# Local-score normalisation and expert-score scaling on VectorE instead of GpSimd

## The chip, the cores and the metric

The kernel runs on one core of one Trainium2 chip. The metric is device time in microseconds (us) of one execution; the median of three runs stands for a kernel.

## The reference

Three layers run one after the other on a batch of 4 sequences of 768 tokens. The first is a local attention with 8 heads of 64: each chunk of 32 queries sees 8 memory keys, 16 keys to the left, its own 32 and 8 to the right. The second is a mixture of four causal attention experts over the 512 outputs of the first; each token keeps its two best experts by a gate. The third is a low-rank mix over the sequence followed by a feed-forward block of 2048.

```
scores = scale * np.matmul(q_c, k_full.transpose(0, 1, 3, 2))
scores = scores - np.max(scores, axis=-1, keepdims=True)
a = np.exp(scores)
a = a / (np.sum(a, axis=-1, keepdims=True) + 1e-09)      # local attention
...
a = np.exp(scores)                                       # expert e, causal, 768 x 768
a /= a.sum(-1, keepdims=True) + 1e-09
ye = a @ v @ wo[e]
...
out += mask[..., None] * w[:, :, kk:kk + 1] * ye         # the token's two gates
...
u = x + h.transpose(0, 2, 1)                             # h = low-rank mix
ch = np.maximum(u @ w_ch1, 0.0) @ w_ch2
```

## The kernel before

**Stages.** From the start to about 450 us of the profiled span the core runs both attentions, interleaved; behind that come the feed-forward products. The change touches the first stage alone.

**Rounds.** `rnd` writes one round of the attention. It takes up to three pieces of work: the scores of one expert block (`scores`: batch `b`, pair of experts `pr`, block `i` of 128 queries against `(i+1)*128` keys), the values of the block of the round before (`turn_scores`, `values`), the scores of one local unit (`local_load`, `local_scores`: a pair of heads and half a sequence, in two groups `qd` of three windows) and the turning and values of the local unit of the round before (`local_turn`, `local_values`). There are 12 rounds for each of the 4 batches, and 6 rounds ahead of them with local units alone. Projections (`qk_proj`, `v_proj`) fill the rounds. In the last batch the first steps of the feed-forward block (`fuse_w1`, `load_w2`, `early`) fill them too.

**Chain of one local group.** TensorE writes three score tiles of 128x96 (line 417). VectorE adds the band and takes the minimum (line 421), ScalarE takes the exponential with its sum `ss` (line 424), VectorE makes `rs = 1/(ss + 1e-9)` (lines 427 and 428), GpSimd multiplies the 128x288 tile `a` by `rs` (line 429). One round later TensorE transposes `a` (line 437), VectorE or ScalarE copies it out of PSUM (line 439) and TensorE multiplies by the values (line 665). There are 64 such groups.

**Chain of one expert block.** TensorE writes the scores of two experts (lines 548, 549, 551). VectorE takes the maximum (lines 566 or 575), ScalarE the exponential with its sum `su` (line 560), VectorE makes `1/(su + 1e-9)` (lines 579, 580), GpSimd multiplies each of the two tiles `ac` (128 by 128 to 768) by it and by the token's gate (line 582). One round later TensorE transposes it (line 600), the copies `ath` out of PSUM (line 603) alternate between ScalarE and VectorE, and TensorE multiplies by the values (line 665). There are 48 blocks, so 96 scalings. The gate `g` (lines 519 to 535) is made on VectorE, eight times.

**What else GpSimd and VectorE do there.** GpSimd also copies the halves `kd`, `kl` of the expert keys to the other partitions (line 496, 64 times). VectorE also makes the low parts `xl` of the local outputs (line 456), on which the projections wait, `qs` and `kl` (lines 488, 494), and the output of the mix, `z` (line 657).

**What sets the order.** The program text is written round by round; the framework's scheduler then gives each engine one queue in a fixed order, by priority and a model of durations, and the engines meet through semaphores. An instruction that waits holds all that is behind it on its engine. Only the runs of narrow matmuls (`part`, line 665) are kept together by explicit dependencies. PSUM is short: `s` and `tp` share two buffers, `sc`, `tpc`, `pyt`, `pz` share another two.

Of the kernel before, what the change touches and what calls it, by code (L numbers as in the profile page):

```python
# [22 lines left out]
GK = NMEM + LEFT + GQ + RIGHT  # L23
# [69 lines left out]
def tile_chunk_attention__moe_attention__mixer(  # L93
# [19 lines left out]
    nc = tc.nc  # L113
# [217 lines left out]
    with ExitStack() as p1:  # L331
# [77 lines left out]
        def local_scores(u, qd):  # L409
            b, hp, hf = u  # L410
            w = half[u]
            s = ps.tile([128, 3, GK], F32, name="s", **TL)
            a = lwk.tile([128, 3, GK], F32, name="a")
            nm = sm.tile([128, 3], F32, name="nm")
            ss = sm.tile([128, 3], F32, name="ss")
            for j in range(3):
                nc.tensor.matmul(s[:, j, :], w["q"][:, qd * 3 + j], w["k"][:, qd * 3 + j], start=True, stop=True)  # L417
            for j in range(3):
                g = hf * NG // 2 + qd * 3 + j
                bd = band_s[:, 0 if g == 0 else 2 if g == NG - 1 else 1]  # L420
                nc.vector.tensor_tensor_reduce(a[:, j, :], s[:, j, :], bd, op0=ALU.add, op1=ALU.min,  # L421
                                               scale=-scale, scalar=-NEG_LOCAL, accum_out=nm[:, j:j + 1])
            for j in range(3):
                nc.scalar.activation(a[:, j, :], a[:, j, :], AF.Exp, bias=nm[:, j:j + 1], scale=-1.0,  # L424
                                     accum_out=ss[:, j:j + 1])
            rs = sm.tile([128, 3], F32, name="rs")
            nc.vector.tensor_scalar(rs, ss, 1e-9, None, op0=ALU.add)
            nc.vector.reciprocal(rs, rs)  # L428
            nc.gpsimd.tensor_mul(a, a, rs[:, :, None].to_broadcast([128, 3, GK]))  # L429
            w["a"][qd] = a  # L430

        def local_turn(u, qd):
# [108 lines left out]
        def score_mm(s, off, b, e, i, base):  # L541

            q = qs[b, e, i // 3][:, i % 3 * 128:(i % 3 + 1) * 128]
            for hf in range(i // 3 + 1):
                w = HALF if hf < i // 3 else (i % 3 + 1) * 128
                o = off if hf == 0 else base
                last = hf == i // 3
                nc.tensor.matmul(s[:, o:o + w], q, kl[b, e, hf][:, :w], start=True, stop=False)  # L548
                nc.tensor.matmul(s[:, o:o + w], q, kd[b, e, hf][:, :w], start=False, stop=not last)  # L549
                if last:  # L550
                    nc.tensor.matmul(s[:, o + w - 128:o + w], identb_s, tri_s, start=False, stop=True)

        def scores(b, pr, i, between=None):
            n = (i + 1) * 128
            nm = sm.tile([128, 2], F32, name="nmc")
            su = sm.tile([128, 2], F32, name="su")
            aa = [cw.tile([128, S], F32, name="ac", bufs=NAC) for _ in range(2)]

            def expo(h, src):
                nc.scalar.activation(aa[h][:, :n], src, AF.Exp, bias=nm[:, h:h + 1], scale=1.0, accum_out=su[:, h:h + 1])  # L560

            if i < 3:
                s = ps.tile([128, 2, 512], F32, name="sc", **TC)
                for h in range(2):
                    score_mm(s[:, h], 0, b, 2 * pr + h, i, 0)
                nc.vector.tensor_reduce(nm, s[:, :, :n], axis=AX.X, op=ALU.max, negate=True)
                for h in range(2):
                    expo(h, s[:, h, :n])
                if between:
                    between()  # L570
            else:
                for h in range(2):
                    s = ps.tile([128, 1024], F32, name="sc", **TC)
                    score_mm(s, 128, b, 2 * pr + h, i, 512)
                    nc.vector.tensor_reduce(nm[:, h:h + 1], s[:, 128:128 + n], axis=AX.X, op=ALU.max, negate=True)  # L575
                    expo(h, s[:, 128:128 + n])
                    if h == 0 and between:
                        between()
            nc.vector.tensor_scalar(su, su, 1e-9, None, op0=ALU.add)
            nc.vector.reciprocal(su, su)  # L580
            for h in range(2):
                nc.gpsimd.tensor_scalar(aa[h][:, :n], aa[h][:, :n], su[:, h:h + 1],  # L582
                                        gates[b, i // 3][:, i % 3, 2 * pr + h:2 * pr + h + 1], op0=ALU.mult, op1=ALU.mult)
            a_ts[b, pr, i] = aa

# [83 lines left out]
        def rnd(new=None, old=None, s_unit=None, o_unit=None, fill1=(), fill2=(), down=None):  # L669
            if s_unit:  # L670
                local_load(s_unit)
                local_scores(s_unit, 0)
# [6 lines left out]
            if new:  # L679
                scores(*new, between)  # L680
            if not turned:
                between()
            if s_unit:
                local_scores(s_unit, 1)
# [96 lines left out]
        for b in range(B):  # L781
# [7 lines left out]
            for r, (pr, i) in enumerate(ROUNDS):  # L789
                n = (FILL0 if b == 0 else FILL)[r] if work else 0  # L790
# [263 lines left out]
```

## Time and profile before

| | us |
|---|---|
| median of 3 runs | 863.04 (862.87 to 864.9) |
| the profiled execution | 859.0 |
| its span, first to last instruction | 857.2 |
| TensorE busy with matmuls | 811.0 (95%) |
| VectorE busy | 630.5 (74%) |
| ScalarE busy | 494.8 (58%) |
| GpSimd busy | 168.0 (20%) |

The mean granted TensorE clock is 0.984 of full speed. Busy time is the share of the span in which an engine executes. A share of the whole span mixes stages; the section of rows gives the engines by stage. GpSimd's 168.0 us lie almost wholly in the first 450 us.

### The profile page before, as it was taken

To read this page: it belongs to the slowest core of one execution; us is meant where nothing else is said; L and a number is where in the kernel's file an instruction comes from. 1 tells how busy PE (TensorE), PEld (TensorE's weight loads), DVE (VectorE), ACT (ScalarE), POOL (GpSimd) and SP (SyncE) were. 2 spreads that over 40 slices of the span, in tenths; PEclk is the share of its full clock that TensorE was granted. 3 is DMA by queue.
4 is the path that set the end of the run, shared out by engine and by line. 5 is a ranking of instruction groups with operands and counts; after the bars stand their busy time and mean duration, and the time that the engine had idled before them with its cause. 6 is when DMAs were issued, how large, how long until landed. Compare 5 with 4: busy or idle time off the path is not lost.

```text
span 857.2 us, 18057 instructions
## 1 busy us (share of the span) xinstructions
PE 811.0 (95%) x6404; PEld 727.1 (85%) x6404; DVE 630.5 (74%) x1997; ACT 494.8 (58%) x1464; POOL 168.0 (20%) x254
## 2 busy tenths in 40 slices
PE   7889999999999998889979999999999999999995
PEld 5778999889987897768767878999989989899995
DVE  5687766577767766899536899989578495775947
ACT  3587766577656755656434566656464454645533
POOL 5334343344433424222110000000000000000002
PEclk8799999999999999999999999999999999999999
DMA  9644422133222201253206744301203012030101
GB/s 246 181 122 112 111 76 75 57 98 107 50 68 76 85 1 45 86 182 108 74 19 200 226 159 148 99 25 50 75 1 123 1 50 75 1 124 1 62 38 50
DMA packets 59627, 74.74 MB, mean 87 GB/s; under 512 B 29456, under 2 KB 34064, under 8 KB 58768
## 3 DMA queue, kind: packets, MB, share of 16 engines
q1 hardware_dynamic: 59536, 73.57, 27.9%
q8 instruction: 51, 0.84, 0.4%
q14 instruction: 40, 0.33, 0.1%
HBM read 57.83 MB, written 15.73 MB: 86 GB/s over the span
## 4 chain that ended last, share of the span: by engine, by line
PE 72%; DVE 9%; DMA 8%; ACT 6%; issue 3%; SPq 1%; POOL 1%; DVEq 0%; ACTq 0%; POOLq 0%
PE acc L934 23%; PE ph L285 14%; PE t L665 7%; PE pqk L468 5%; DMA raw<-in_w 4%; PE pv L508 3%; PE s L417 3%; PE tpc L600 3%; PE po L301 3%; PE sc L548 3%; PE sc L549 2%; PE tp L437 2%; DMA part<-o 2%; ACT a L424 1%; ACT ac L560 1%
## 5 line engine op out<-in xcount | busy, mean ns | idle before, releaser
L934 PE MATMUL acc<-xhi,sw 128*128 128x256 f32 x1008 | 191.6, 283 | 0.9 <-ACT xhi L876 0.9
L934 PEld LDWEIGHTS acc<-xhi,sw 128*128 128x128 f32 x1008 | 160.6, 189 | 8.1 <-ACT xhi L876 2.2
L934 PE MATMUL acc<-xlo,sw 128*128 128x256 f32 x504 | 139.2, 283 | 0.0
L873 DVE TENSOR_TENSOR sx<-t 128x256 f32<-128x256 f32 x180 | 67.8, 420 | 72.0 <-ACT t L866 72.0
L866 ACT ACTIVATE t<-ph 128x512 f32<-128x512 f32 x72 | 43.0, 597 | 121.2 <-PE ph L285 121.2
L582 POOL TENSOR_SCALAR ac<-ac,su,g 128x128 f32<-128x128 f32 (+5 forms) x96 | 70.0, 738 | 157.7 <-DVE su L580 102.7
L934 PEld LDWEIGHTS acc<-xlo,sw 128*128 128x128 f32 x504 | 95.4, 189 | 2.6
L925 POOL TENSOR_TENSOR pt<-pt,cp 128x512 f32<-128x512 f32 x3 | 6.4, 2155 | 408.6 <-DVE xlo L877 408.6
L876 ACT CAST xhi<-sx 128x256 fp32r<-128x256 f32 x210 | 76.0, 407 | 13.8 <-PE acc L934 6.2
L424 ACT ACTIVATE a<-a,nm 128x96 f32<-128x96 f32 x192 | 69.9, 367 | 22.9 <-DVE nm L421 22.2
L877 DVE TENSOR_TENSOR xlo<-sx,xhi 128x256 fp32r<-128x256 f32 x210 | 80.1, 421 | 3.8 <-ACT xhi L876 3.3
L560 ACT ACTIVATE ac<-sc,nmc 128x128 f32<-128x128 f32 (+5 forms) x96 | 60.4, 632 | 35.3 <-DVE nmc L575 20.3
L285 PE MATMUL ph<-zh,wp_l 128*128 128x512 f32 x192 | 61.0, 398 | 1.0 <-ACT zh L273 1.0
L417 PE MATMUL s<-k_t,qbd 128*128 128x96 f32 x384 | 56.3, 284 | 5.3 <-DMA k_t<-in_kw 4.0
L600 PE MATMUL tpc<-ident_s,ac 128*128 128x128 f32 x336 | 54.0, 279 | 7.0 <-ACT ath L603 2.9
L285 PE MATMUL ph<-zh,wp_h 128*128 128x512 f32 x192 | 60.3, 394 | 0.0
L429 POOL TENSOR_TENSOR a<-a,rs 128x288 f32<-128x288 f32 x64 | 42.6, 668 | 82.1 <-DVE rs L428 23.2
L417 PEld LDWEIGHTS s<-k_t,qbd 128*128 128x128 f32 x384 | 51.2, 200 | 8.1 <-issue 4.0
L285 PE MATMUL ph<-zl,wp_h 128*128 128x512 f32 x176 | 56.6, 393 | 0.0
L548 PE MATMUL sc<-kl,qs 128*128 128x384 f32 (+2 forms) x144 | 51.3, 357 | 2.6 <-DVE z L657 1.4
L421 DVE CUSTOM_DVE_ANT_0 a<-s,band_s 128x96 f32<-128x96 f32 x192 | 40.2, 252 | 16.6 <-PE s L417 13.9
L600 PEld LDWEIGHTS tpc<-ident_s,ac 128*128 128x128 f32 x336 | 39.5, 143 | 13.0 <-issue 6.2
(174 smaller groups left out, 2038.7 us busy)
## 6 DMA issues: line engine op xcount, KB each, us to landing
raw<-in_w SPq DMA_DIRECT2D x64, 256.0 KB, 3.5
k_t<-in_kw SPq DMA_DIRECT2D x32, 288.0 KB, 3.4
v_t<-in_vw SPq DMA_DIRECT2D x32, 288.0 KB, 3.2
qbd<-in_qT SPq DMA_DIRECT2D x64, 96.0 KB, 2.8
part<-o SPq DMA_DIRECT2D x24, 256.0 KB, 2.5
pt<-part SPq DMA_DIRECT2D x6, 1024.0 KB, 4.9
out<-pt SPq DMA_DIRECT2D x24, 256.0 KB, 2.5
zf<-zs SPq DMA_DIRECT2D x8, 512.0 KB, 4.7
```

What stands on the lines that cost most here:

```text
L285: nc.tensor.matmul(p, w[f // 4][:, pr, fs], z[:, pr], start=(n == 0), stop=(n == 5))
L417: nc.tensor.matmul(s[:, j, :], w["q"][:, qd * 3 + j], w["k"][:, qd * 3 + j], start=True, stop=True)
L424: nc.scalar.activation(a[:, j, :], a[:, j, :], AF.Exp, bias=nm[:, j:j + 1], scale=-1.0, accum_out=ss[:, j:j + 1])
L548: nc.tensor.matmul(s[:, o:o + w], q, kl[b, e, hf][:, :w], start=True, stop=False)
L560: nc.scalar.activation(aa[h][:, :n], src, AF.Exp, bias=nm[:, h:h + 1], scale=1.0, accum_out=su[:, h:h + 1])
L582: nc.gpsimd.tensor_scalar(aa[h][:, :n], aa[h][:, :n], su[:, h:h + 1], gates[b, i // 3][:, i % 3, 2 * pr + h:2 * pr + h + 1], op0=ALU.mult, ...
L600: nc.tensor.transpose(tp[h][:, j * 128:(j + 1) * 128], aa[h][:, j * 128:(j + 1) * 128], ident_s)
L665: session.append(nc.tensor.matmul(*a, **kw).ins)
L873: nc.vector.tensor_tensor(x, t[:, p[0], p[1]], t[:, q[0], q[1]], op=op)
L876: nc.scalar.copy(hi, x)
L877: nc.vector.tensor_sub(lo, x, f32(hi))
L934: nc.tensor.matmul(acc[n][:, m], w[:, ms], x, start=(f == FA and u == 0 and m == 0), stop=(f == NF - 2 and u == 2 and m == 1))
```

## The change

Two instructions change engine. The multiplication of the local scores by the reciprocal of their sum, and the scaling of the expert scores by reciprocal and gate, are issued on VectorE with the same operands.

```
@@ -426,7 +426,7 @@
             rs = sm.tile([128, 3], F32, name="rs")
             nc.vector.tensor_scalar(rs, ss, 1e-9, None, op0=ALU.add)
             nc.vector.reciprocal(rs, rs)
-            nc.gpsimd.tensor_mul(a, a, rs[:, :, None].to_broadcast([128, 3, GK]))
+            nc.vector.tensor_mul(a, a, rs[:, :, None].to_broadcast([128, 3, GK]))
             w["a"][qd] = a
@@ -579,7 +579,7 @@
             nc.vector.tensor_scalar(su, su, 1e-9, None, op0=ALU.add)
             nc.vector.reciprocal(su, su)
             for h in range(2):
-                nc.gpsimd.tensor_scalar(aa[h][:, :n], aa[h][:, :n], su[:, h:h + 1],
+                nc.vector.tensor_scalar(aa[h][:, :n], aa[h][:, :n], su[:, h:h + 1],
                                         gates[b, i // 3][:, i % 3, 2 * pr + h:2 * pr + h + 1], op0=ALU.mult, op1=ALU.mult)
             a_ts[b, pr, i] = aa
```

Since the scheduler orders the queues anew, other instructions shift too. GpSimd's queue keeps its other work in the order it had. Two places on VectorE's queue show what happens. The first is the end of the sixth gate, at 266 to 269 us of the trace of before (`g_4116`, `den_4128` are the gate; `a_4213`, `rs_4225`, `rs_4307` belong to local groups, `su_4065` and `ac_` to an expert block; + is after, - is before):

```order
 L579 TENSOR_SCALAR su_4065<-su_4065 128x2
 L530 SCALAR_TENSOR_TENSOR g_4116<-cnt_4125,g_4116 128x12
+L429 TENSOR_TENSOR a_4213<-a_4213,rs_4225 128x288
 L580 RECIPROCAL su_4065<-su_4065 128x2
+L532 TENSOR_REDUCE den_4128<-g_4116 128x3
 L427 TENSOR_SCALAR rs_4307<-ss_4297 128x3
-L532 TENSOR_REDUCE den_4128<-g_4116 128x3
+L582 TENSOR_SCALAR ac_4066<-ac_4066,su_4065,g_3524 128x128
+L582 TENSOR_SCALAR ac_4067<-ac_4067,su_4065,g_3524 128x128
+L533 TENSOR_SCALAR den_4128<-den_4128 128x3
 L428 RECIPROCAL rs_4307<-rs_4307 128x3
```

The multiplications stand between the small steps of the gate, and the copy `at_4233` (line 439), which stood ahead of `rs_4225` before, stands behind `rs_4307` now.

The second is a little ahead of it, in the queue in front of `xl_3945`, a low part on which a projection waits:

```order
+L579 TENSOR_SCALAR su_3949<-su_3949 128x2
+L580 RECIPROCAL su_3949<-su_3949 128x2
+L582 TENSOR_SCALAR ac_3950<-ac_3950,su_3949,g_3524 128x384
+L582 TENSOR_SCALAR ac_3951<-ac_3951,su_3949,g_3524 128x384
 L456 TENSOR_TENSOR xl_3945<-t_3927,xh_3944 128x384
-L566 TENSOR_REDUCE nmc_3948<-sc_3952 128x2
 L421 ISA a_4213,nm_4214<-s_4212,band_s_106 128x96
```

The reciprocal of this block and both its scalings were moved ahead of `xl_3945` and of the local minimum of `s_4212`.

## Rows read from the trace of the kernel before

**Rows 1.** Busy us, share and instructions of each engine, from the page.

```profile
PE 811.0 (95%) x6404; PEld 727.1 (85%) x6404; DVE 630.5 (74%) x1997; ACT 494.8 (58%) x1464; POOL 168.0 (20%) x254
```

**Rows 2.** Busy time by stage: from:to, length, engines, granted clock, DMA share, GB/s.

```profile
core 0: us, PE busy (x) PEld busy (x) DVE busy (x) ACT busy (x) POOL busy (x), PEclk, DMA share, GB/s
43.00:364.00 321.00, 304.39 (x3083) 277.50 (x3082) 231.61 (x926) 214.60 (x750) 124.83 (x200) 1.00 0.27 78
364.00:450.00 86.00, 77.52 (x502) 62.08 (x500) 60.68 (x140) 44.01 (x107) 16.28 (x18) 0.96 0.29 95
450.00:857.00 407.00, 394.16 (x2608) 359.66 (x2606) 312.45 (x815) 215.88 (x526) 6.39 (x3) 1.00 0.23 79
```

**Rows 3.** The chain that ended last, shares of the span, from the page.

```profile
PE 72%; DVE 9%; DMA 8%; ACT 6%; issue 3%; SPq 1%; POOL 1%; DVEq 0%; ACTq 0%; POOLq 0%
```

**Rows 4.** The chain, 43 to 364 us: start, us, what (DVE's ends, POOL's pieces).

```profile
43.94 0.26 DVE a L421
...
100.53 0.67 POOL a L429
...
102.56 1.53 POOL ac L582 x2
...
360.48 0.34 DVE d_t L129
```

**Rows 5.** Lines 429, 582: min/median/max ns; who waited for them; page group (idle before last).

```profile
L429 POOL TENSOR_TENSOR a<-a,rs x64: 664/666/700, 12.6 to 302.3; 128x288 f32<-128x288 f32 x64
...
  PEld tp L437: 0.5, 1
```

```profile
L582 POOL TENSOR_SCALAR ac<-ac,su,g x96: 442/764/1576, 64.2 to 434.2; 128x128 f32<-128x128 f32 x16, 128x256 f32<-128x256 f32 x16, 128x384 f32<-128x384 f32 x16, 128x512 f32<-128x512 f32 x16
...
  DVE a L421: 1.0, 1
  PEld tpc L600: 0.5, 2
```

```profile
L582 POOL TENSOR_SCALAR ac<-ac,su,g 128x128 f32<-128x128 f32 (+5 forms) x96 | 70.0, 738 | 157.7 <-DVE su L580 102.7
```

**Rows 6.** VectorE instructions of like shape: count, busy us, mean ns, idle before.

```profile
L877 DVE TENSOR_TENSOR xlo<-sx,xhi 128x256 fp32r<-128x256 f32 x210 | 80.1, 421 | 3.8 <-ACT xhi L876 3.3
L970 DVE TENSOR_TENSOR pt<-pt,acc 128x512 f32<-128x512 f32 x22 | 14.5, 681 | 0.0
L603 DVE COPY ath<-tpc 128x768 f32<-128x768 f32 x8 | 7.6, 954 | 6.0 <-PE tpc L600 6.0
L603 DVE COPY ath<-tpc 128x128 f32<-128x128 f32 x8 | 2.3, 284 | 3.9 <-PE tpc L600 3.9
```

**Rows 7.** Casts on VectorE from one SBUF tile, line 366: min/median/max ns.

```profile
L366 DVE CAST wqk_h<-raw x4: 426/508/1118, 4.3 to 10.2; 128x512 fp32r<-128x512 f32 x4
L366 DVE CAST wvg_h<-raw x4: 297/298/694, 14.0 to 18.5; 128x260 fp32r<-128x260 f32 x4
```

**Rows 8.** Multiplications and scalings by stage: POOL's busy us (instructions), lines 429, 582.

```profile
43.00:364.00 321.00, 35.94 (x54) 1.00 0.27 78
```

```profile
43.00:364.00 321.00, 56.15 (x82) 1.00 0.27 78
```

**Rows 9.** Line 427 on VectorE: its group with the mean; its min/median/max.

```profile
L427 DVE TENSOR_SCALAR rs<-ss 128x3 f32<-128x3 f32 x64 | 16.0, 250 | 14.9 <-ACT a L424 14.7
```

```profile
L427 DVE TENSOR_SCALAR rs<-ss x64: 140/170/1192, 11.2 to 301.8; 128x3 f32<-128x3 f32 x64
```

**Rows 10.** The timeline at 267 us: start, us, engine, line (POOL, then DVE).

```profile
267.22 0.67 POOL L429 TENSOR_TENSOR a<-a,rs 128x288 f32<-128x288 f32 x1 [1.51 <-DVE g L530]
```

```profile
267.31 0.60 DVE L427 TENSOR_SCALAR rs<-ss 128x3 f32<-128x3 f32 x1
```

**Rows 11.** A wait of the whole span: us in total, times, longest.

```profile
PEld t L665 <- DVE ath L603: 8.2, 11, 1.9
```

**Rows 12.** Busy time from 364 to 407 us, columns as in group 2.

```profile
364.00:407.00 43.00, 40.40 (x226) 32.22 (x225) 39.91 (x99) 26.62 (x67) 11.06 (x12) 0.96 0.44 144
```

More of the change, by code (lines that the diff above doesn't have):

```diff
@@ L428, in local_scores @@
             nc.vector.reciprocal(rs, rs)
-            nc.gpsimd.tensor_mul(a, a, rs[:, :, None].to_broadcast([128, 3, GK]))
+            nc.vector.tensor_mul(a, a, rs[:, :, None].to_broadcast([128, 3, GK]))
             w["a"][qd] = a
@@ L581, in scores @@
             for h in range(2):
-                nc.gpsimd.tensor_scalar(aa[h][:, :n], aa[h][:, :n], su[:, h:h + 1],
+                nc.vector.tensor_scalar(aa[h][:, :n], aa[h][:, :n], su[:, h:h + 1],
                                         gates[b, i // 3][:, i % 3, 2 * pr + h:2 * pr + h + 1], op0=ALU.mult, op1=ALU.mult)
```

## The prediction

> **What bounds the kernel now.** I read the busy times first, then the same by stage, then the chain of work that ended last, then the two lines that change. TensorE is busy 95% of the span [rows 1]. By stage it is 304.4 of 321 us from 43 to 364, 77.5 of 86 us from there to 450, and 394.2 of 407 us behind [rows 2]. So TensorE is the bound, and all that the attention could give back between 43 and 450 us is its idle time, 16.6 + 8.5 = 25.1 us. GpSimd is busy 124.8 of the 321 us and VectorE 231.6, or 72% [rows 2]. Of the chain, 72% of the span is on TensorE, 9% on VectorE and 1% on GpSimd [rows 3]. Between 43 and 364 us I added up its pieces: 141 on VectorE, from the one at 43.94 to the one at 360.48, are 40.8 us, 12.7% of the stretch; the multiplications on GpSimd are two pieces, 0.67 and 1.53 us [rows 4]. VectorE is thus the second engine of the path and GpSimd hardly on it. That shows from the other side too: TensorE's weight loads waited for line 429 once, 0.5 us, and for line 582 twice, 0.5 us, and VectorE waited for line 582 once, 1.0 us [rows 5]. GpSimd itself mostly waits: it was idle 157.7 us ahead of line 582, 102.7 of it until a reciprocal of line 580 [rows 5]. One round lies between these products and the transposes that read them, and this round covers GpSimd's slowness.
>
> **What goes from GpSimd.** The 64 multiplications have a median of 666 ns, the 96 scalings one of 764 ns [rows 5]. Nearly all of it was cover. What can be given back on the path is the two pieces, 2.2 us, since VectorE's own time for them is counted below.
>
> **What comes to VectorE.** The trace has no such instruction on VectorE, so I bound it by its likes. A multiplication has two inputs in SBUF: 256 columns take 421 ns and 512 columns, one input from PSUM, 681 ns [rows 6], or 1.016 ns for each column more, so 288 columns make 421 + 32 x 1.016 = 453 ns; 64 of them are 29.0 us. A scaling reads one SBUF tile. The casts from one SBUF tile take 298 ns for 260 columns and 426 ns at best for 512 [rows 7], 0.51 ns a column; from 128 to 768 columns this is 230, 296, 361, 426, 491 and 557 ns, 2,361 ns in sum, and 16 of each are 37.8 us. The upper end is a copy that reads PSUM, 284 ns for 128 columns and 954 for 768 [rows 6]; on a straight line between them the six sizes make 3,714 ns, and 16 of each 59.4 us. I take 37.8, since casts share source and destination with the scalings, and keep 59.4 for the range. Together VectorE gets 66.8 us. Between 43 and 364 us there are 54 of the 64 and 82 of the 96 [rows 8], 24.5 us and, by GpSimd's time for them, 37.8 x 56.15 / 70.0 = 30.3 us (70.0 us in all, [rows 5]): 54.8 us.
>
> **What VectorE gets back.** Line 427, the addition on 128x3, has a median of 170 ns but a mean of 250 and a worst case of 1192 [rows 9]. The timeline shows why: at 267.31 it takes 0.60 us, beginning just behind a GpSimd multiplication of 0.67 us and ending with it [rows 10]. A small VectorE instruction on SBUF tiles stands still while GpSimd works. The excess is 64 x 80 ns = 5.1 us for this line. Other lines on SBUF tiles show the same now and then, and the copies of line 496 stay on GpSimd and go on doing it, so I take 5 to 10 us in all, 8 for the sum. Page SBUF — State Buffer, section Who interferes with whom, of the Trainium skill says that the two engines share a port pair, which a VectorE instruction with two SBUF inputs or in a two-port mode and a GpSimd instruction hold in turn, each for its whole length. By that rule, the trace agrees where small instructions meet GpSimd, and both kinds of new instruction would be among those that can be held up by the copies of line 496; I have no row for that, and leave it to the upper end.
>
> **What of it lies on the path.** From 43 to 364 us VectorE goes from 231.6 to 231.6 + 54.8 - 8 = 278 us, 87% of the stretch; its idle time halves, from 89 to 43 us. A piece laid on VectorE at random hits a stretch where the path is on VectorE 12.7% of the time as things are; with half the idle time left to absorb it, I let the rate double to 25% by the last piece and take the mean, 19%: 54.8 x 0.19 = +10.4 us. If the rate stayed it would be +7.0. The hits are of a kind that exists already: the copies `ath` make TensorE's weight loads wait 8.2 us in 11 places now [rows 11], and the two scalings in front of `xl` hold up 2 x 0.36 us what a projection waits for. No new wait for another engine comes with the change: each product needs only the reciprocal ahead of it on its own queue, and `a` and `ac`, whose sums VectorE had waited for already. What queues behind it is the next minimum, maximum, copy or low part, and TensorE behind that. Off go the 2.2 us of GpSimd on the path, and of the 8 us given back the part that lay on it: six pieces of line 427 are on the chain, 2.4 us where six medians would be 1.0, so about 1.4, and about 0.9 for other lines. Sum for this stretch: +10.4 - 2.2 - 2.3 = +5.9 us. From 364 to 450 us there are 14 scalings, mostly long ones, some 6 us; from 364 to 407 VectorE is busy 39.9 of 43 us [rows 12], with no room, but from 407 on it has plenty and the feed-forward work there can wait. I put +1. Ahead of 43 us ten multiplications stand under loads from memory: nothing. Behind 450 us nothing changes. Total: **+6.9 us**, or 859.0 + 6.9 = 865.9 for a profiled execution like this one. The runs' median is 4.0 us above the profiled execution, so 863.0 + 6.9 = **870**.
>
> **Rivals.** *Faster:* GpSimd was a brake. Its hop and its holding-up of VectorE go, and VectorE's idle time, 89 us in the stretch, swallows all 54.8: -2.2 - 2.3 and nothing against it, 858.5. For it speak the bursts at the gates: at 267 us the chain runs through VectorE, where two multiplications and two scalings come in (2 x 0.45 + 2 x 0.23 = 1.4 us) and at least the 0.43 us of line 427 go. Against it, even this burst gets longer. Page GPSIMD Engine Reference, section 4.1, of the Trainium skill recommends VectorE for elementwise products, GpSimd being about twice as slow with two inputs. By that rule the change would be right; the trace agrees in the sign, 666 ns against my 453, a ratio of 1.5, but the longer time was under cover. *No change:* the slack of one round hides the new VectorE time as it hid GpSimd's, hits and gifts cancel (7.0 at the old rate less 4.5, plus nothing at the end): 863 to 865. Against it, VectorE's queue is not only this chain's: the maxima, copies and low parts behind a product have less than a round of slack. *VectorE becomes the bound:* the scalings run at the upper price, 59.4 us. Then 24.5 + 47.6 = 72 us come in between 43 and 364, VectorE is at 92%, its idle time 25 us, and the rate would end near 12.7 x 89 / 25 = 45%; the mean, 29%, gives +21, less 4.5, plus 3 for the crowded 43 us behind 364: +19, 882. Its point of decision is the scaling's duration: above some 600 ns on average it is this case. *The order does it:* the scheduler's new queues could cost or give a few us by themselves; the diff shows the maxima and `xl` swapped around the products, and TensorE's queue swapped in as many places. It has no sign of its own and widens the others.
>
> **How the numbers follow.** About 0.3%, 2.6 us, is what a measurement of this kernel can tell from no change. Chances: the forecast, slower by 3 to 14 us, 0.47; VectorE as the bound, beyond that, 0.14; no change 0.21; faster 0.18. So slower 0.61, same 0.21, faster 0.18. The range leaves out a tenth at either end: 858.5 is the faster rival's time and 882 that of the bound, so 858 to 884.
>
> **What would show it.** After the change VectorE's busy time should be 630.5 + 66.8 - 8, about 689 us, GpSimd's 168.0 - 42.6 - 70.0, about 55. Line 429 should take near 453 ns and line 582 between 230 and 557. Line 427 should lose its long cases. The chain between 43 and 364 us should hold more than 41 us on VectorE, and TensorE's waits for VectorE (`ath`, `at`, `xl`, `nm`) should grow by several us while its busy time stays at 811. I am wrong if TensorE's idle time before 450 us doesn't grow, or if the time is lost behind 450 us.

## The result, and the profile after

The changed kernel takes **870.27 us** (median of 4 runs, 870.05 to 873.47), the kernel before 863.17 in the same comparison: a ratio of **1.0087, 95% interval 1.006 to 1.0114**, slower by about 7.5 us. A later comparison of the same two kernels gave 1.0142 (1.0111 to 1.0172), 871.58 against 859.63, about 12 us. The two intervals only just touch, so the loss is known to some 7 to 12 us and no better. The execution shown here took 873.47 us with a span of 871.4, some 3 us above its median. The one of before lies 4.0 us under its own. So of the 14.2 us between the two spans about half are owed to which executions were recorded, and what is read below from a pair of traces is held against the medians.

The page of the kernel after: busy us, share and instructions of each engine; the shares of the chain that ended last; the group of the scalings (busy us, mean ns of one | idle before). They answer to [rows 1], [rows 3] and the page row of [rows 5].

```profile
PE 817.7 (94%) x6404; PEld 731.5 (84%) x6404; DVE 682.0 (78%) x2157; ACT 495.5 (57%) x1464; POOL 58.2 (7%) x94
PE 67%; DVE 14%; DMA 8%; ACT 7%; issue 3%; SPq 1%; POOL 0%; DVEq 0%; ACTq 0%; POOLq 0%
L582 DVE TENSOR_SCALAR ac<-ac,su,g 128x128 f32<-128x128 f32 (+5 forms) x96 | 45.2, 514 | 1.0
```

The work went where it was sent: GpSimd has 109.8 us and 160 instructions less, VectorE 51.5 us and 160 more. VectorE's share of the chain rose from 9 to 14%. TensorE, the bound, shows two things. Its idle time grew from 46.2 to 53.7 us, and its busy time grew too, by 6.7 us, for the same 6404 matmuls.

**Where the time was lost.** The last 310 us are mostly the products of line 934. The row of its weight loads (min/median/max ns, first to last start), first before, then after:

```profile
L934 PEld LDWEIGHTS acc<-xhi,sw x1008: 186/188/193, 536.6 to 847.6; 128*128 128x128 f32 x168
```

```profile
L934 PEld LDWEIGHTS acc<-xhi,sw x1008: 186/188/193, 551.1 to 862.0; 128*128 128x128 f32 x168
```

The first is 14.5 us later and the last 14.4: nothing is lost from there on. To find the places ahead of it I used a mark that stands once in each round, the copy `yT` of line 618, and took its start in each kernel less its start in the kernel before (its **lag**). The first and last of the 48, before and after:

```profile
L618 ACT COPY yT<-t x48: 239/264/267, 69.1 to 444.6; 128x128 f32<-128x128 f32 x48
```

```profile
L618 ACT COPY yT<-t x48: 245/266/269, 71.9 to 459.3; 128x128 f32<-128x128 f32 x48
```

The lag is 2.8 us at the first copy and 14.7 at the last. Rounds 1 to 38 take 291.5 us instead of 282.2. The same rounds in both traces (from:to, length, PE, PEld, DVE, ACT, POOL busy, granted clock, DMA share, GB/s), before and then after; this pair answers to [rows 2], since fixed times hold different work in the two kernels:

```profile
69.10:351.30 282.20, 271.24 (x2755) 248.19 (x2754) 200.35 (x772) 186.08 (x643) 110.20 (x175) 1.00 0.26 74
351.30:444.60 93.30, 82.71 (x555) 67.44 (x555) 68.67 (x177) 49.12 (x127) 19.43 (x24) 0.96 0.30 101
```

```profile
71.90:363.40 291.50, 275.88 (x2757) 251.06 (x2757) 238.18 (x891) 186.75 (x640) 31.20 (x56) 0.99 0.26 71
363.40:459.30 95.90, 84.64 (x555) 68.64 (x555) 76.03 (x197) 48.76 (x127) 2.47 (x4) 0.95 0.30 98
```

In rounds 1 to 38 VectorE has 37.8 us more, 82% of the stretch instead of 71%, and the rounds are 9.3 us longer: 25% of what was added. Of the 9.3 us, 4.6 are TensorE's busy time, the rest its idle time. A second execution of the changed kernel (the same queues) takes 288.9 us there, 6.7 more than before: 4.3 of idle and 2.4 of busy time. So the added idle time repeats, and the two executions differ in TensorE's busy time.

**What one place looks like.** The timeline of VectorE between the copies `yT` of rounds 34 and 35, behind a reciprocal of line 580 (start, us, engine, line, operation), before and then after:

```profile
328.65 0.17 DVE L580 RECIPROCAL su<-su 128x2 f32<-128x2 f32 x1
328.85 0.55 DVE L488 SCALAR_TENSOR_TENSOR qs<-pqk,qs 64x384 fp32r<-64x384 f32 x1
329.43 0.82 DVE L603 COPY ath<-tpc 128x640 f32<-128x640 f32 x1
```

```profile
338.22 0.17 DVE L580 RECIPROCAL su<-su 128x2 f32<-128x2 f32 x1
338.42 1.27 DVE L582 TENSOR_SCALAR ac<-ac,su,g 128x768 f32<-128x768 f32 x2
339.72 0.55 DVE L488 SCALAR_TENSOR_TENSOR qs<-pqk,qs 64x384 fp32r<-64x384 f32 x1
340.31 0.82 DVE L603 COPY ath<-tpc 128x640 f32<-128x640 f32 x1
```

The two scalings put everything behind the reciprocal back by 1.30 us, the copy `ath` among it, which empties the PSUM buffer that TensorE's next score matmuls need. TensorE stood idle 1.01 us there before and 2.61 after. By the trace the wait after ended with ScalarE's copy of the other half, 0.3 us behind VectorE's, so not all of the difference is the scalings'.

**A second price, in some executions.** In that idle stretch TensorE was busy 1.39 of 4.0 us. Right behind it the granted clock fell to 0.58, that is for most of it to the lower of its two levels, 1.2 GHz. The windows of after, then those of the second execution:

```profile
338.00:342.00 4.00, 1.39 (x13) 1.19 (x12) 3.85 (x7) 2.52 (x4) 0.00 (x0) 1.00 0.28 102
342.50:346.00 3.50, 3.50 (x34) 2.90 (x34) 1.92 (x6) 0.82 (x5) 0.00 (x0) 0.58 0.00 0
```

```profile
338.00:342.00 4.00, 1.43 (x15) 1.15 (x13) 3.87 (x6) 2.24 (x4) 0.00 (x0) 1.00 0.17 64
342.00:345.50 3.50, 3.50 (x41) 3.13 (x41) 2.71 (x9) 1.51 (x7) 0.00 (x0) 1.00 0.00 0
```

The next 32 value matmuls took 3.38 us, in the second execution 2.02. There TensorE had stood idle 2.58 us at the same place, and the clock stayed at 1.00. So the fall came behind a wait, but a wait like it came without a fall; what decides is not shown. The chains of the two, start, us, what:

```profile
342.56 3.38 PE t L665 x32
```

```profile
342.04 2.02 PE t L665 x32
```

At the first gates it fell in both executions. From 52 to 62 us the chain of after is almost unbroken on VectorE, new multiplications among the gate's small steps. A little later six score matmuls take 1.61 us where six took 0.64 before:

```profile
56.97 0.36 DVE a L429
57.33 0.41 DVE rs L427
57.74 0.02 issue
57.77 0.17 DVE rs L428
57.94 0.05 DVE lg L511
57.99 0.61 DVE a L429
...
64.12 1.61 PE s L417 x6
```

```profile
64.00:76.00 12.00, 10.34 (x83) 8.71 (x83) 9.82 (x52) 8.72 (x41) 0.00 (x0) 0.79 0.28 76
```

Before, this stretch has 1.00. In the second execution of the changed kernel it has 0.59.

### The profile page after: what moved, and what is told of

Same layout as the page of the kernel before. It is cut to its first block, busy times and chain, and to the rows that moved or that the text cites. A ratio compares the mean times of both kernels' runs of the same rounds, so it can differ in the third digit from the quotient of the medians.

```text
span 871.4 us, 17777 instructions
## 1 busy us (share of the span) xinstructions
PE 817.7 (94%) x6404; PEld 731.5 (84%) x6404; DVE 682.0 (78%) x2157; ACT 495.5 (57%) x1464; POOL 58.2 (7%) x94
## 4 chain that ended last, share of the span: by engine, by line
PE 67%; DVE 14%; DMA 8%; ACT 7%; issue 3%; SPq 1%; POOL 0%; DVEq 0%; ACTq 0%; POOLq 0%
PE acc L934 23%; PE ph L285 13%; PE t L665 7%; PE pqk L468 5%; DMA raw<-in_w 3%; PE po L301 3%; PE pv L508 3%; PE s L417 3%; PE tpc L600 3%; PE sc L548 2%; PE sc L549 2%; DMA part<-o 2%; ACT ac L560 1%; PE tp L437 1%; DVE ac L582 1%
## 5 line engine op out<-in xcount | busy, mean ns | idle before, releaser
L876 ACT CAST xhi<-sx 128x256 fp32r<-128x256 f32 x210 | 76.1, 408 | 14.4 <-DVE sx L873 7.1
L665 PE MATMUL t<-ath,vt 128*64 128x128 f32 x672 | 47.8, 283 | 2.7 <-DVE ath L603 2.6
L421 DVE CUSTOM_DVE_ANT_0 a<-s,band_s 128x96 f32<-128x96 f32 x192 | 40.0, 252 | 10.8 <-PE s L417 10.3
L575 DVE TENSOR_REDUCE nmc<-sc 128x1 f32<-128x512 f32 (+2 forms) x48 | 39.2, 821 | 9.7 <-PE sc L551 9.2
L582 DVE TENSOR_SCALAR ac<-ac,su,g 128x128 f32<-128x128 f32 (+5 forms) x96 | 45.2, 514 | 1.0
```

Source lines behind the costliest of these rows:

```text
L582: nc.vector.tensor_scalar(aa[h][:, :n], aa[h][:, :n], su[:, h:h + 1], gates[b, i // 3][:, i % 3, 2 * pr + h:2 * pr + h + 1], op0=ALU.mult, ...
L665: session.append(nc.tensor.matmul(*a, **kw).ins)
L876: nc.scalar.copy(hi, x)
```

## The experiments

The theories: the loss is VectorE's load, in proportion (A); it is the scheduler's new order (B); it is the load, but only in crowded places (D); or it is the place of the products in VectorE's queue (E). Against all of them works the relief, that GpSimd had been a brake (C). Ratios are to the kernel before in the same comparison.

### Each half alone

```
local_only:  L429  nc.gpsimd.tensor_mul    -> nc.vector.tensor_mul
expert_only: L582  nc.gpsimd.tensor_scalar -> nc.vector.tensor_scalar
```

> Half of the change: only the 64 multiplications of the local scores (line 429) go to VectorE, the 96 scalings (line 582) stay on GpSimd. In the changed kernel the 64 took 30.9 us of VectorE and the 96 took 49.3 us. Theory A (VectorE's added time on the path sets the loss of 7.1 us): a share of 30.9 of 80.2, about +2.7 us, 866. Theory B (the scheduler's new queues set it, not the load): no proportion, anything from -4 to +8 us. Theory C (GpSimd holding up VectorE is a brake that the change takes off): the local multiplications hold up line 427 just behind them, so this half is faster than before, 860 to 862.

> The other half: only the 96 scalings of the expert scores (line 582) go to VectorE. Theory A: a share of 49.3 of 80.2, about +4.4 us, 867.5, and the two halves add up to the whole, +7.1. Theory B: no proportion; the halves don't add up. Theory C: slower than before by more than A says, since GpSimd's local multiplications still hold up a fuller VectorE, 868 to 870.

Measured: `local_only` 862.28 us, ratio **1.0006** (0.998 to 1.0031); `expert_only` 872.42 us, ratio **1.0132** (1.0103 to 1.0161). No loss is shown for the local multiplications; the scalings carry it. The same rounds 1 to 38, first `local_only`, then `expert_only`:

```profile
70.50:353.60 283.10, 271.76 (x2755) 248.24 (x2753) 214.66 (x818) 185.45 (x641) 82.83 (x129) 1.00 0.27 73
```

```profile
73.30:366.30 293.00, 276.07 (x2755) 250.78 (x2753) 225.14 (x846) 186.46 (x643) 60.69 (x103) 0.99 0.26 71
```

The first adds 14.3 us of VectorE and 0.9 us of time (6%), the second 24.8 and 10.8 (44%). The second rate is a high one: this execution lies 4.1 us above its median, and 4.8 of its 10.8 us are TensorE's busy time. The ratios say the same of whole executions: 0.5 us (-1.7 to 2.7) lost for 19.8 us more on VectorE, and 11.4 us (8.9 to 13.9) for 32.3. Load in proportion, with one rate for all, is out. One sign also misleads: VectorE's pieces of the chain between 43 and 364 us, by a count alike for all traces (which comes to 38.5 us before, where the prediction's own came to 40.8), are 68.3 us after, 60.3 in `expert_only`, and 59.0 in `local_only`, which loses nothing. A chain that runs through an engine more often isn't a longer one.

### Both steps taken out, and the load without the relief

```
neither:            lines 429 and 582 removed
vector_load_added:  before, and behind each of the two on GpSimd, on the scratch tile dum
+   dl = dum[:, :3 * GK].rearrange("p (j k) -> p j k", k=GK)
+   nc.vector.tensor_mul(dl, dl, rs[:, :, None].to_broadcast([128, 3, GK]))
...
+   nd_ = min(n, 480)
+   nc.vector.tensor_scalar(dum[:, :nd_], dum[:, :nd_], su[:, h:h + 1],
+                           gates[b, i // 3][:, i % 3, 2 * pr + h:2 * pr + h + 1], op0=ALU.mult, op1=ALU.mult)
```

> Both steps are left out, so local scores stay without normalisation and expert scores without normalisation and gate: GpSimd loses 112.6 us of work and VectorE gains none. It tells what GpSimd's two steps cost before. Theory A: they were nearly all under cover; what comes back is two pieces of the chain, 2.2 us, and some of the 8 us that VectorE stood still: 2 to 5 us faster, 858 to 861. Theory B: within 3 us either way. Theory C: more than 6 us faster.

> The kernel before, with GpSimd doing all that it did, and VectorE doing beside it the same number of instructions on a scratch tile, behind the same reciprocals (64 of 128x288, 96 of 128 by 128 to 480): VectorE's load without any relief from GpSimd. Theory A: at least the whole loss and what the relief was worth, +8 to +13 us, 871 to 876. Theory B: again no proportion, -4 to +8. Theory C: much slower than the changed kernel, since GpSimd still holds VectorE up, over 876.

Measured: `neither` 854.05 us, ratio **0.9911** (0.9883 to 0.994); `vector_load_added` 895.43 us, ratio **1.0382** (1.0342 to 1.0422).

`neither` sets the whole price of the two steps before at 7.7 us. Its lag is 0.5 us at round 1, -0.3 at round 38, -6.0 at round 39 and again -2.9 at round 48; its span is 4.3 us shorter. In 38 rounds, with most of these products, GpSimd cost 0.8 us. In round 39 ScalarE's `yT` stood behind a cast that waited for a load, and in `neither` it stands ahead of it (ScalarE's timeline, before and then `neither`; the line numbers of `neither` are 4 lower there):

```profile
364.04 0.43 ACT L126 ACTIVATE d_t<-raw 128x256 f32<-128x256 f32 x1 [0.61 <-DMA raw<-in_w]
364.50 0.27 ACT L618 COPY yT<-t 128x128 f32<-128x128 f32 x1
```

```profile
358.48 0.26 ACT L614 COPY yT<-t 128x128 f32<-128x128 f32 x1
```

So what the trace shows of the 7.7 us may be an order in the last batch and no slowness of GpSimd, and half of that jump is given back by round 48. Neither was tried by itself, and where the rest of the 7.7 us comes from stays open.

`vector_load_added` costs about three to four times what the change costs. It shows what happens when both engines do this work at once: each holds the other up. GpSimd's widest scaling in the kernel before, then the same scaling (line 586) and the two-input multiplication that was added on VectorE (line 433) in this kernel:

```profile
L582 POOL TENSOR_SCALAR ac<-ac,su,g 128x768 f32<-128x768 f32 x16 | 15.6, 985 | 29.5 <-DVE su L580 20.2 <-ACT hh L293 5.2 <-DVE lg L511 4.1
```

```profile
L586 POOL TENSOR_SCALAR ac<-ac,su,g 128x768 f32<-128x768 f32 x16 | 20.2, 1267 | 31.0 <-DVE su L584 30.8
L433 DVE TENSOR_TENSOR dum<-dum,rs 128x288 f32<-128x288 f32 x64 | 35.6, 555 | 0.8
```

985 ns become 1267, and VectorE's multiplication takes 555 where it takes 482 in the changed kernel. By page SBUF — State Buffer, section Who interferes with whom, of the Trainium skill, the two engines take a shared port pair in turn; the trace agrees, 1267 against 985 ns. Since the added instructions also slow GpSimd, this run doesn't measure VectorE's load alone, and the difference to the changed kernel isn't the relief alone either.

### Once more, and batch by batch

```
expert_mid_batches:  L582  (nc.vector if b in (1, 2) else nc.gpsimd).tensor_scalar
expert_end_batches:  L582  (nc.vector if b in (0, 3) else nc.gpsimd).tensor_scalar
expert_first_batch:  L582  (nc.vector if b == 0 else nc.gpsimd).tensor_scalar
expert_last_batch:   L582  (nc.vector if b == 3 else nc.gpsimd).tensor_scalar
```

> The changed kernel itself, beside the three that follow, on the same chip: every theory expects +7 us again (ratio 1.006 to 1.011 was measured). It gives the halves and the variants a whole to be compared with, and a second trace, since single executions of one kernel differ by some us.

> The expert scalings (line 582) on VectorE for batches 1 and 2 only, 48 of the 96; the rest, and all local multiplications, on GpSimd. All scalings on VectorE cost 11.4 us (expert_only). Theory D (the loss arises where VectorE's queue is crowded: the first batch, where the lag of the last outputs of a round behind the kernel before grew to 8.4 us of 18 in expert_only's trace, and the last batch with the feed-forward decoding, 5.4 more; between lie 4.4): 4.4/18 of 11.4, about +3 us. Theory A (in proportion to VectorE's added time, wherever it is): 48 of 96, +5.7 us.

> The complement: the expert scalings on VectorE for batches 0 and 3 only. Theory D: about +8.5 us. Theory A: +5.7 us. Theory B (the order of the queues alone): the two parts don't add up to 11.4.

> The kernel before with the 24 scalings of batch 0 alone on VectorE. Theory of crowded places (the loss falls where VectorE's queue is already full: the first gates' burst and rounds 5 to 13, then the last batch): most of what batches 0 and 3 lost together, so +5 to +9 us, ratio 1.006 to 1.010. Rival, loss in proportion to the load: a quarter of 11.4 us, +2 to +4, ratio 1.002 to 1.005. Rival, the loss is one of the scheduler's new order and belongs to no place: anything from 0 to +11.

> The kernel before with the 24 scalings of batch 3 alone on VectorE. Crowded places: the rest of what batches 0 and 3 lost together, +2 to +5 us (ratio 1.002 to 1.006), and the sum with batch 0 alone is near the +11 us of the two together. Proportional: +2 to +4 as well, but then the sum is 6 and not 11. If it costs nothing, the feed-forward work of the last batch fills in.

| kernel | scalings on VectorE | median | ratio (95%) | lag at round 1, 12, 24, 38, 48 |
|---|---|---|---|---|
| the changed kernel | 96, and the local ones | 870.27 | 1.0087 (1.006 to 1.0114) | 2.8, 5.2, 6.9, 12.1, 14.7 |
| the same again | 96, and the local ones | 871.58 | 1.0142 (1.0111 to 1.0172) | 3.6, 6.3, 7.9, 10.3, 12.8 |
| `expert_only` | 96 | 872.42 | 1.0132 (1.0103 to 1.0161) | 4.2, 8.4, 10.0, 15.0, 18.2 |
| `expert_first_batch` | 24 | 865.77 | 1.0052 (1.0028 to 1.0077) | 2.9, 7.2, 7.2, 7.3, 9.0 |
| `expert_mid_batches` | 48 | 864.75 | 1.0063 (1.0037 to 1.0089) | 3.6, 3.6, 5.1, 7.5, 10.3 |
| `expert_last_batch` | 24 | 863.12 | 1.0015 (0.9991 to 1.0039) | 3.4, 3.4, 3.4, 4.2, 6.4 |
| `expert_end_batches` | 48 | 869.92 | 1.0133 (1.0108 to 1.0158) | 4.3, 7.8, 7.8, 8.4, 11.0 |
| `local_only` | 0 | 862.28 | 1.0006 (0.998 to 1.0031) | 1.4, 1.3, 2.3, 2.3, 3.8 |
| `late_gpsimd` (next section) | 0 | 862.45 | 1.0011 (0.9991 to 1.0031) | 4.0, 4.0, 4.0, 4.0, 3.0 |

The lag follows the edit. Where the first batch alone is moved it grows from 2.9 to 7.2 us in rounds 1 to 12 and then stands still for 26 rounds; where the middle batches are moved it stands at 3.6 for 12 rounds and grows from 13 on, mostly at rounds 13, 25 and 34 to 35. So the loss is made where the scalings are moved. It isn't even: 4.3 us for the 24 of the first batch, 3.9 us for the 48 of the middle ones. In rounds 38 to 48 the kernels with anything moved lose 1.5 to 3.2 us, those with no scaling moved there too, so the last batch's are not shown to cost anything, and their ratio includes 1.

The lag alone doesn't tell the scalings' time from the new order, since the order of the other instructions changes in the same stretch and nowhere else: between 64 and 150 us of the trace of before for the first batch, between 164 and 333 us for the middle ones. One place of `expert_mid_batches` tells them apart. From 319 to 332 us the queues of VectorE, ScalarE and TensorE have the order of before, with the scalings put in and nothing else. There, between the copies of rounds 33 and 34 (timelines, before and then `expert_mid_batches`):

```profile
320.62 0.17 DVE L580 RECIPROCAL su<-su 128x2 f32<-128x2 f32 x1
321.50 0.69 DVE L603 COPY ath<-tpc 128x512 f32<-128x512 f32 x1 [0.71 <-PE tpc L600]
322.25 0.92 PE L665 MATMUL t<-at,v_t 96*64 96x64 f32 x24
```

```profile
327.07 0.17 DVE L580 RECIPROCAL su<-su 128x2 f32<-128x2 f32 x1
327.27 1.14 DVE L582 TENSOR_SCALAR ac<-ac,su,g 128x640 f32<-128x640 f32 x2
328.32 0.68 DVE L603 COPY ath<-tpc 128x512 f32<-128x512 f32 x1
329.06 0.92 PE L665 MATMUL t<-at,v_t 96*64 96x64 f32 x24 [0.49 <-DVE ath L603]
```

Before, VectorE stood idle 0.71 us ahead of the copy `ath`. The pair of scalings fills this gap and 0.37 us more: seen from the reciprocal, the copy begins that much later, and TensorE, which by the trace waits for it, 0.36 us later. Here it is VectorE's time and no order. How much of the whole loss is of this kind isn't shown.

The start of the lag isn't the edit's. `late_gpsimd` runs the instructions of before in the same order on every engine, from the first to the last, and is 4.0 us late at round 1. About 4 us were lost by 37 us, among the first loads and projections. From there its lag stays between 3.9 and 4.0 us for 38 rounds:

```profile
L618 ACT COPY yT<-t x48: 242/264/272, 73.1 to 447.6; 128x128 f32<-128x128 f32 x48
```

So a start lag of 0 to 4 us is chance, and a change of the lag in rounds 1 to 38 is not; in rounds 38 to 48 the same queues differ by 1.0 us.

Two accounts don't close. Middle and end batches are all 96 scalings, and their losses add up to +1.96%, where `expert_only` has +1.32%: by the expectations that is the sign of the order, theory B. First, middle and last add up to 1.0052 + 1.0063 + 1.0015, that is +1.30%, as `expert_only` has it (+1.32%). But first and last are +0.67%, and the two together measured +1.33%, while their trace shows hardly more lag than that of the first batch (6.7 us from first to last copy against 6.1). That `expert_end_batches` loses twice what its parts lose stays open, and with it how large a part the order has.

### The place in the queue, and the order alone

```
late_vector: the changed kernel, with both products written at the end of the round
+   late.append(lambda: nc.vector.tensor_mul(a, a, rs[:, :, None].to_broadcast([128, 3, GK])))
...
+   late.append(lambda: [nc.vector.tensor_scalar(aa[h][:, :n], aa[h][:, :n], su[:, h:h + 1],
+                        gates[b, i // 3][:, i % 3, 2 * pr + h:2 * pr + h + 1], op0=ALU.mult, op1=ALU.mult)
+                        for h in range(2)])
...
+   for f in late:
+       f()
late_gpsimd: the same with nc.gpsimd for nc.vector
```

> The changed kernel with both kinds of product written at the end of their round instead of right behind their reciprocals, so that in VectorE's queue they come behind that round's maxima, copies and low parts; the readers are a round later, as before. VectorE's load is the same as in the changed kernel. Theory E (position: a product ahead of a copy or a low part is what TensorE waits for): most of the loss goes, -1 to +3 us against the kernel before. Theory A (VectorE's load as such): +6 to +8 us as the changed kernel.

> The kernel before with the two products, still on GpSimd, written at the end of each round. This changes only the place of the instructions in the text, and so the scheduler's order. If the order alone moves the time by several us, the ratio leaves 0.997 to 1.003, and the comparison of the late products on VectorE has to be read against this one. If the order costs little and the load on VectorE costs much, 0.998 to 1.002.

Measured: `late_vector` 872.31 us, ratio **1.0147** (1.0123 to 1.017); `late_gpsimd` 862.45 us, ratio **1.0011** (0.9991 to 1.0031). The text was changed, the queues hardly. The traces give the order in which each engine ran its instructions: `late_gpsimd` has that of the kernel before on every engine, so it is that kernel once more and no test of a new order. In `late_vector` VectorE's queue, products included, is that of the changed kernel from round 13 on, but for two steps of one gate. Over all rounds a scaling stands at most three places behind its reciprocal in 72 of the 96 cases, in the changed kernel in 78. The scheduler put the products back to where they had been. So theory E wasn't tested: what the place of a product in VectorE's queue costs stays open. Against the order alone speaks `local_only`, in which several hundred instructions of VectorE, ScalarE and TensorE change places between 9 and 304 us and no loss is shown.

### What a scaling costs

```
one_scalar: the changed kernel, L582
-   nc.vector.tensor_scalar(aa[h][:, :n], aa[h][:, :n], su[:, h:h + 1],
-                           gates[b, i // 3][:, i % 3, 2 * pr + h:2 * pr + h + 1], op0=ALU.mult, op1=ALU.mult)
+   nc.vector.tensor_scalar(aa[h][:, :n], aa[h][:, :n], su[:, h:h + 1], None, op0=ALU.mult)
```

> The changed kernel with the scaling by the reciprocal alone; the multiplication by the token's gate is left out of the expert scores, so each scaling reads one scalar per partition and not two. If the second scalar and its multiplication make the scalings dear, line 582 takes 230 to 557 ns, VectorE's busy time falls by some 11 us, and at about 20 to 25% of that on the path the time falls 2 to 3 us below the changed kernel: ratio to before 1.008 to 1.012. If a scaling costs what it does whatever it multiplies by, line 582 stays at 343 to 678 ns and the ratio at 1.012 to 1.016.

Measured: 872.87 us, ratio **1.013** (1.01 to 1.0161). The scalings by size, the narrowest and the widest, of after and then of this kernel (busy us, mean ns of one | idle):

```profile
L582 DVE TENSOR_SCALAR ac<-ac,su,g 128x768 f32<-128x768 f32 x16 | 10.2, 678 | 0.2
...
L582 DVE TENSOR_SCALAR ac<-ac,su,g 128x128 f32<-128x128 f32 x16 | 4.8, 343 | 0.2
```

```profile
L582 DVE TENSOR_SCALAR ac<-ac,su 128x768 f32<-128x768 f32 x16 | 9.2, 617 | 0.2
...
L582 DVE TENSOR_SCALAR ac<-ac,su 128x128 f32<-128x128 f32 x16 | 3.8, 282 | 0.2
```

Without the second scalar the widest and the narrowest are 61 ns shorter, the other sizes 56 to 72. That is about half of what I had missed, so neither expectation of the duration holds. The line's busy time falls from 45.2 to 39.4 us and the kernel is no faster. A saving of 6 us at the rate of 20 to 25% would be little over 1 us, which lies inside the interval.

## Why the prediction was right, step by step

**The sign and the size.** The case of the forecast, slower by 3 to 14 us, came in, by 7 us and again by 12. That 870.27 lies so near 870 is luck: the second comparison is 5 us away from it, and one term of the sum was nearly empty, as told below. The faster rival, at 858.5, fell. So did "no change" (863 to 865) and VectorE as the bound (882).

**The bound and the slack.** TensorE was the bound and GpSimd's slowness was under cover: `neither` gains 0.8 us in 38 rounds. VectorE had no such cover for the scalings, as `expert_only` shows. For the local multiplications it had: `local_only` shows no loss, and for this half the rival "no change" was right.

**The durations.** Line 429 was right: 453 ns predicted, a median of 457 and a mean of 482, 30.9 us for 29.0. Line 582 was mis-sized:

```profile
L429 DVE TENSOR_TENSOR a<-a,rs x64: 430/457/1334, 12.0 to 312.1; 128x288 f32<-128x288 f32 x64
L582 DVE TENSOR_SCALAR ac<-ac,su,g x96: 340/540/681, 66.6 to 447.9; 128x128 f32<-128x128 f32 x16, 128x256 f32<-128x256 f32 x16, 128x384 f32<-128x384 f32 x16, 128x512 f32<-128x512 f32 x16
```

It is 343 to 678 ns by size for 230 to 557, 49.3 us as a sum of durations for 37.8. The price per column was right, (678 - 343) / 640 = 0.52 ns against 0.51 from the casts [rows 7]; the fixed part was some 120 ns too low. A cast takes no scalar per partition, and the one-scalar form shows about half of the 120; the other half is unexplained. Part of it was taken back: two neighbours overlap, and the line's busy time is 45.2 us.

**What VectorE got back.** Line 427 lost its long cases, as said: its mean fell from 250 ns [rows 9] to 173, 4.9 us in all. With the gate's lines 526 and 535 (2.5 and 1.1) and two others (1.4) it is 9.9 us, for 8 predicted.

```profile
L427 DVE TENSOR_SCALAR rs<-ss x64: 154/166/474, 11.6 to 311.7; 128x3 f32<-128x3 f32 x64
```

VectorE's busy time rose by 51.5 us, not 58.8. Added up instruction by instruction in the two traces, the durations rose by 73.2 us; the other 21.7 us overlap with neighbours (line 582 at 330.34 us is followed by the next instruction 1.05 us later, though its two durations sum to 1.22).

**What of it lay on the path.** +5.9 predicted for 43 to 364 us; rounds 1 to 38 lost 9.3 us, 6.7 in the second execution (10.3 - 3.6). +1 predicted for the last stretch; 2.6 and 2.5, but kernels with no scaling moved there show -1.0 to 2.8. Nothing behind 450 us, as said. The step that failed is the rate. I laid all of VectorE's new time on the path at 19%, as if pieces fell at random. The whole came out near it (18 and 25% of the 37.8 us), but the two kinds are not alike: 6% for the local multiplications, 44% for the scalings. One half alone, I would have forecast badly. What makes the scalings dear is only argued: they come in pairs of up to 1.27 us, behind the reciprocal and ahead of copies for which PSUM buffers wait, while a local multiplication is 0.48 us. The place ahead of round 34's copy shows the kind of loss, a pair longer than the idle time ahead of the copy, and not its share. The place in the queue wasn't tested, since `late_vector` didn't move it.

**The relief.** I took 2.2 + 2.3 = 4.5 us as given back in this stretch. `neither`, which has all of it and no new load, gains 0.8 us between rounds 1 and 38. That term was nearly empty. The hits, predicted at 10.4, are then 10.1 and 7.5 us by the two executions (9.3 and 6.7 with the 0.8 added), and part of that is TensorE at the lower clock, which the sum didn't have. In the second execution two errors cancel, hits and relief both too high; in the first the hits fit and the sum for this stretch is 3.4 us low.

**TensorE's busy time.** It was to stay at 811 and rose to 817.7, and to 817.0 in the second execution. This step was missing: in places the granted clock is lower than before, and the same matmuls take longer. It is almost half of the growth of the span after, nearly as large as the added idle time (7.5 us). That the waits bring the lower clock is argued from where it fell, and the wait without a fall speaks against a fixed rule.

**TensorE's waits for VectorE** grew by less than said: all of them together are 21.7 us before, 25.8 after and 23.0 in the second execution. The rest of its added idle time ends with other engines by the trace, ScalarE among them (10.4, 12.9 and 13.0 us), which waits for VectorE in its turn. Three of the waits, after (us in total, times, longest):

```profile
ACT ac L560 <- DVE nmc L575: 26.1, 28, 3.0
PEld t L665 <- DVE ath L603: 8.8, 12, 1.5
PE t L665 <- DVE ath L603: 7.7, 9, 1.8
```

Before they were 20.3, 8.2 ([rows 11]) and 6.6 us. ScalarE's wait for the maxima of line 575 grew by 5.8 us.

**The order** was given no sign. `local_only` has its queues ordered anew too and measures as equal, but `expert_end_batches` and round 39 of `neither` show that single places may move by several us. No run has the new order without the new load, so its part of the loss stays open.

No version here beats the kernel before. `local_only` equals it, and the 7.7 us of `neither` are no version, since the work must be done somewhere.

## What to carry to other kernels

Before moving work from a slow engine, ask who waits for it, and for the fast one: a GpSimd step with a round of slack cost 0.8 us in 38 rounds, and the same scalings, 0.5 us each instead of 0.74, cost 11 us on an engine that the bound waits for. Size each kind of moved instruction, and its hits on the path, by itself: the mean over two kinds was near here and each of the two was off. Put a mark that occurs once a round beside the same mark in the other trace: it tells a loss at its place from the start's chance, which a difference of two spans doesn't. And before you read a variant that moves a line in the text, see in its trace whether the queue moved: in both variants here it hardly did.

## What the runs showed of the hardware

A VectorE scaling by two per-partition scalars took 343 ns for 128 columns and 678 for 768, by one scalar 282 and 617: the second scalar costs 61 ns at both ends (56 to 72 between them), and the columns 0.52 ns each. With both engines multiplying, a GpSimd scaling of 768 columns went from 985 to 1267 ns and a VectorE multiplication of 288 took 555 (on a scratch tile) where it takes 482. A wait can be followed by a lower clock: behind 4.0 us in which TensorE worked 1.39, its granted clock was 0.58, and 32 matmuls took 3.38 us; behind 4.0 us in which it worked 1.43, in another execution, it was 1.00, and they took 2.02. And the same queues, run again, were 4.0 us later after the first loads and then kept this distance to 0.1 us for 38 rounds.
